# Grouped-query decode attention on one Trainium2 core: first K tile in quarters, shorter TensorE register code, a second unused matmul per V tile

## The chip, the cores and the metric

The kernel runs on one NeuronCore of a Trainium2 chip. The metric is device time of the whole kernel in microseconds (us), the median over several executions.

## The reference

One query position, 32 query heads, 8 K/V heads, 65,536 keys of 128 numbers, all bfloat16:

```python
B, Hq, Hkv, Sq, Sk, D = 1, 32, 8, 1, 65536, 128
k = jnp.repeat(k, rep, axis=1); v = jnp.repeat(v, rep, axis=1)
scores = jnp.einsum("bhqd,bhkd->bhqk", q, k) * D ** -0.5
p = _softmax(scores, axis=-1)
return jnp.einsum("bhqk,bhkd->bhqd", p, v)
```

K and V together are 268.4 MB, each byte read once. The output is 8 KB.

## The kernel before

Each of the 8 groups (one K/V head, 4 query heads) has two K tiles and two V tiles of 128 partitions x 256 keys x 128 numbers, 8.39 MB each. The kernel keeps three tiles on chip: one V tile and two K tiles. SyncE issues all loads into one queue, in the order k(0,0), k(0,1), k(1,0), v(0,0), k(1,1), v(0,1), k(2,0), ... where v(0,1) is the second V tile of group 0. A load can be issued only when the tile before it in its buffer has been used:

```python
k_lo = {0: [0, 128], 1: [0, 64, 128, 192]}
def load_k(g, b):
    SP.wait((s_sc, 16 * g - 8 + 8 * b if g else 0))     # that K buffer's scores are done
    ...
    cuts = [0, 128, SL] if g == 0 else [0, 64, 128, 192, SL] if (g, b) == (G - 1, 1) else [0, SL]
    for lo, hi in zip(cuts, cuts[1:]):
        load(k, g, b, 1 + b, s_k[b, lo], lo, hi)

def load_v(g, b):
    done = 2 * (2 * g + b)
    ...                                  # last tiles in pieces (cut)
        values_done(done)                # waits for the matmuls of the V tile before
        load(v, g, b, 0, s_v[0])
```

VectorE transposes a K tile in four quarters (64 keys each). Each quarter gives TensorE two *parts* of eight matmuls. The part loop lives in registers:

```python
with block("pe_part"):
    nc.regs_alu(r_q, r_q, 8, op=ALU.add)
    for r, bits in r_q_bits.items():              # 8, 112, 24, 96
        nc.regs_alu(r, r_q, bits, op=ALU.bitwise_and)
    ...
    take(pe, PE, s_kt, 1)
    ...                                           # eight matmuls into acc (cut)
    nc.regs_alu(r_n, r_q, 56, op=ALU.bitwise_and)
    nc.br_cmp(r_n, 56, "pe_part", "pe_skip", "IS_LT", engines=only)
...
with block("pe_values"):
    ...
    for ch in range(4):                           # quarters of a V tile, 16 wide (512-column) matmuls each
        ...
        if ch == 1:
            i.then_inc(s_vc, 1)
            pe.matmul(out=pt[0:16, :], lhsT=et[:, 0, 0:16], rhs=et[:, 0, :], start=True, stop=True)  # unused
```

After a K tile's parts, TensorE does the V tile of the group before. The very last V tile arrives in eight pieces; TensorE ends with 8 wide matmuls for the piece that ends at key 224 of each partition, and 32 small ones for the last 32 keys.

## Time and profile before

The median of the first three runs was 631.91 us (631.76 to 631.94). The profiled execution took 631.43 us.

From the page of the kernel before: busy time and share of the span per engine; then the DMA row (busy tenths of the sixteen DMA engines in 40 equal slices of the span); then the input queue (packets, MB, share of sixteen engines' span).

```profile
span 629.5 us, 7271 instructions
PE 348.6 (55%) x2126; PEld 137.9 (22%) x2126; DVE 345.3 (55%) x154; ACT 34.4 (5%) x26; POOL 9.7 (2%) x42
...
DMA  8999999999999999999999999999999999999995
...
q1 hardware_dynamic: 6656, 268.45, 98.8%
```

The DMA engines are the bound: they are busy 98.8% of the span, while TensorE and VectorE work 55% of the time. If the stream's pace stays what it is (434 GB/s, below), this kernel can win only at three places: where the stream starts, where it has a hole, and in the tail after the last bytes. So look for a hole. VectorE waits for each K tile to land, so the starts of its transposes show the stream's pace. The timeline of VectorE, before (start us, duration us, engine, line, operation; in brackets the idle time before it):

```profile
100.39 8.77 DVE L369 STREAM_TRANSPOSE io<-io 128x4096 uint32<-128x4096 uint32 x2 [14.13 <-DVEq L119]
...
140.51 17.42 DVE L369 STREAM_TRANSPOSE io<-io 128x4096 uint32<-128x4096 uint32 x4 [4.42 <-DVEq L119]
...
179.19 8.77 DVE L369 STREAM_TRANSPOSE io<-io 128x4096 uint32<-128x4096 uint32 x2 [21.09 <-DVEq L119]
```

From one K tile to the next is two loads (a V and a K tile). From 140.51 to 179.19 it is 38.68 us, and so on to the end of the run, which is 434 GB/s (16.78 MB in 38.68 us). But from 100.39 to 140.51 it is 40.12: 1.4 us more, once. The load between them that matters is v(0,1). The timeline of SyncE's DMA issues, before:

```profile
38.64 0.43 SPq L137 DMA_DIRECT2D io<-in_v_dram  x1
59.50 0.33 SPq L137 DMA_DIRECT2D io<-in_k_dram  x1
97.44 0.33 SPq L137 DMA_DIRECT2D io<-in_v_dram  x1
97.82 0.43 SPq L137 DMA_DIRECT2D io<-in_k_dram  x1
129.21 0.33 SPq L137 DMA_DIRECT2D io<-in_v_dram  x1
```

v(0,1) is issued at 97.44, and the load ahead of it, the last one queued, lands at 100.25. The trace records a completion for each of the sixteen DMA engines. For v(0,1) the first engine completes on time, at 119.21, the last only at 120.99; from then on the engines stay about 1.8 us apart to the end (1.78 at 120.99, 1.67 at 624.87), and the kernel waits for the slowest. Of the first packets of v(0,1), fourteen start by 99.79, and two start at 99.92 and 100.49 and take 2.98 and 3.29 us instead of 2.42. So this is a hole in one or two engines, and the page's DMA rows do not show it.

The tail, in the timeline of TensorE and its followers, before:

```profile
622.30 1.03 PE L254 MATMUL acc<-io,et 128*16 128x512 bf16 x8 [1.36 <-DMA io<-in_v_dram]
...
623.21 2.82 PE L354 MATMUL pf<-io,et 128*4 128x128 bf16 x28
...
626.09 0.39 PE L354 MATMUL pf<-io,et 128*4 128x128 bf16 x4
626.58 0.36 ACT L483 ACTIVATE o<-pf,rl 4x128 bf16<-4x128 f32 x1 [32.53 <-PE pf L354]
```

and the same stretch in windows of 2 us (columns: window, its length, busy us and instructions of PE, PEld, DVE, ACT, POOL; then the granted TensorE clock, which is the share of full speed that TensorE was allowed, the DMA share and GB/s):

```profile
620.00:622.00 2.00, 0.94 (x16) 0.22 (x10) 0.00 (x0) 0.00 (x0) 0.00 (x0) 1.00 1.00 379
622.00:624.00 2.00, 1.70 (x18) 1.13 (x19) 0.62 (x1) 0.00 (x0) 0.00 (x0) 0.53 0.58 198
624.00:626.00 2.00, 2.00 (x25) 1.98 (x23) 0.86 (x4) 0.00 (x0) 0.00 (x0) 0.61 0.06 18
```

The last bytes land at 624.87; TensorE ends at 626.48, 1.61 us later, because its clock was granted only by half from 622.13 to 625.55: the small matmuls start 107 ns apart in that stretch, and 56 ns apart after it.

### The profile page before, as it was taken

The numbers are of one execution on the slowest core, as the hardware profiler recorded it, in microseconds if no ns is written. First come the engines' busy times: TensorE is split into PE (matmuls) and PEld (weight loads), VectorE is DVE, ScalarE is ACT, GpSimd is POOL, SyncE is SP. The second block draws the span as 40 slices with busy tenths as digits, with TensorE's granted clock in tenths as the row PEclk, the third lists the DMA queues.
The fourth block names the chain that finished last, engine by engine and source line by source line (L and its number), as shares of the span: only waits on it lengthen the run. The fifth ranks groups of instructions, "written<-read, shape, count | busy, mean of one in ns | idle before, by whom it ended". The sixth has DMA issues, their size and how long they took to land. (4 is left out here: it accounts for less than half of the span.)

```text
span 629.5 us, 7271 instructions
## 1 busy us (share of the span) xinstructions
PE 348.6 (55%) x2126; PEld 137.9 (22%) x2126; DVE 345.3 (55%) x154; ACT 34.4 (5%) x26; POOL 9.7 (2%) x42
## 2 busy tenths in 40 slices
PE   0776384827628275381854718458183671886435
PEld 0222131312213122130311303123031230332113
DVE  4994846549065590655807557084670946694210
ACT  0000200020000200002000020000200002000100
POOL 2000000000000000000000000000000000000000
PEclk9999596976959789596896968869698695999567
DMA  8999999999999999999999999999999999999995
GB/s 367 433 466 400 466 400 462 404 462 404 462 408 458 408 458 408 458 408 458 408 458 412 454 412 454 416 450 429 437 433 433 441 425 441 401 428 433 433 431 237
DMA packets 6715, 268.48 MB, mean 426 GB/s; under 512 B 825, under 2 KB 1081, under 8 KB 1465
## 3 DMA queue, kind: packets, MB, share of 16 engines
q1 hardware_dynamic: 6656, 268.45, 98.8%
q8 instruction: 1, 0.02, 0.0%
q10 hardware_dynamic: 56, 0.01, 0.0%
q14 instruction: 2, 0.01, 0.0%
HBM read 268.44 MB, written 0.01 MB: 426 GB/s over the span
## 5 line engine op out<-in xcount | busy, mean ns | idle before, releaser
L296 PE MATMUL acc<-io,wz 128*128 x1024 | 268.7, 413 | 192.7 <-PEq L119 185.6
L369 DVE STREAM_TRANSPOSE io<-io 128x4096 uint32<-128x4096 uint32 x64 | 279.6, 4415 | 154.0 <-DVEq L119 154.0
L296 PEld LDWEIGHTS acc<-io,wz 128*128 x1024 | 105.2, 103 | 356.3 <-issue 276.5
L254 PE MATMUL acc<-io,et 128*16 128x512 bf16 x1016 | 68.1, 412 | 20.8 <-PEq L119 19.4
L406 DVE TENSOR_REDUCE mg<-acc 128x1 f32<-128x2048 f32 x8 | 18.3, 2292 | 54.1 <-DVEq L119 54.1
L436 ACT ACTIVATE ex<-acc,nmb 128x2048 bf16<-128x2048 f32 x8 | 15.7, 1967 | 557.6 <-DVE nmb L416 557.6
L254 PEld LDWEIGHTS acc<-io,et 128*16 128x16 bf16 x1016 | 26.2, 94 | 59.2 <-issue 35.3
L248 PE MATMUL pf<-vs,sel 128*4 128x130 f32 (+1 forms) x20 | 5.7, 386 | 54.2 <-PEq L119 54.2
L372 DVE STREAM_TRANSPOSE et<-ex 128x1024 bf16<-128x1024 bf16 x17 | 20.8, 1225 | 22.2 <-SPq L157 12.4
L446 ACT ACTIVATE acc<-wz 128x2560 f32<-128x2560 bf16 (+2 forms) x8 | 16.3, 2040 | 1.0 <-ACT ex L436 0.2
L505 POOL COPY wz<-qT 32x16 bf16<-32x16 bf16 x32 | 6.1, 189 | 514.1 <-PE acc L296 442.8
L408 DVE TENSOR_REDUCE m<-pt 1x4 f32<-1x128 f32 x8 | 2.2, 279 | 21.0 <-DVEq L119 21.0
L248 PEld LDWEIGHTS pf<-vs,sel 128*4 128x4 f32 x20 | 1.2, 83 | 54.7 <-issue 54.7
L380 DVE TENSOR_REDUCE vs<-vy 128x128 f32<-128x512 f32 x9 | 6.1, 681 | 7.6 <-DVEq L119 7.6
L419 DVE TENSOR_TENSOR vy<-acc,sely 128x512 f32<-128x512 f32 x8 | 8.5, 1064 | 0.0
L468 DVE TENSOR_TENSOR vy<-acc,sely 128x512 f32<-128x512 f32 x1 | 0.7, 692 | 12.1 <-PE acc L254 12.1
L321 PE MATMUL pt<-et 128*16 128x512 bf16 x16 | 6.5, 406 | 0.0
L338 PE MATMUL pb<-ident,nrow 1*128 1x1 f32 x8 | 1.6, 200 | 7.5 <-PEq L119 7.5
L336 PE MATMUL pt<-ident,mg 128*1 128x128 f32 x8 | 2.3, 283 | 2.6 <-PEq L119 2.6
L416 DVE COPY nmb<-pb 128x1 f32<-128x1 f32 x8 | 1.3, 158 | 4.0 <-DVEq L119 4.0
L354 PE MATMUL pf<-io,et 128*4 128x128 bf16 x32 | 3.2, 281 | 0.0
L338 PEld LDWEIGHTS pb<-ident,nrow 1*128 1x128 f32 x8 | 1.2, 144 | 8.9 <-issue 8.9
(31 smaller groups left out, 22.9 us busy)
## 6 DMA issues: line engine op xcount, KB each, us to landing
io<-in_v_dram SPq DMA_DIRECT2D x5, 4096.0 KB, 16.8
io<-in_k_dram SPq DMA_DIRECT2D x4, 4096.0 KB, 26.0
io<-in_k_dram SPq DMA_DIRECT2D x4, 2048.0 KB, 40.2
io<-in_v_dram SPq DMA_DIRECT2D x1, 2048.0 KB, 10.8
io<-in_v_dram SPq DMA_DIRECT2D x1, 1024.0 KB, 13.0
io<-in_v_dram SPq DMA_DIRECT2D x3, 256.0 KB, 13.3
io<-in_v_dram SPq DMA_DIRECT2D x2, 128.0 KB, 13.3
io<-in_k_dram SPq DMA_DIRECT2D x13, 48.0
```

The source lines that it names most:

```text
L248: return pe.matmul(out=pf[0:H, 0:w], lhsT=sel[:, :], rhs=vs[:, 0:w], skip_group_check=True, **kw)
L254: return pe.matmul(out=vacc[32 * c:32 * c + 16, :, :], lhsT=et[:, ch // 2, w0:w0 + 16], rhs=io[:, PS * ch + 4 * tt:PS * ch + 4 * tt + 4, : ...
L296: i = pe.matmul(out=bass.AP(acc, r_o, [[2560, P], [1, 512]]), lhsT=bass.AP(wz, r_w + ((2 * s + e) * WB - 4 * u), [[4 * WB, P], [1, P]]), r ...
L321: pe.matmul(out=pt[0:16, :], lhsT=et[:, 0, 0:16], rhs=et[:, 0, :], start=True, stop=True)
L369: dve.transpose(out=part, in_=part).then_inc(s_kt, 2)
L372: dve.transpose(out=et[:, :, :].rearrange("p i n -> p (i n)"), in_=ex[:, 2 * b:2 * b + 2, :].rearrange("p i n -> p (i n)"),).then_inc(s_et, 1)
L380: DV.mark(dve.tensor_reduce(out=vs[:, 0:D], in_=vy[:, :, :], axis=AX.X, op=ALU.add))
L406: dve.tensor_reduce(out=mg[:, :], in_=sc, axis=AX.X, op=ALU.max).then_inc(s_mg, 1)
L419: dve.tensor_tensor(out=vy[:, :, :].rearrange("p d y -> p y d"), in0=vacc, in1=sely[:, :, None].to_broadcast([P, 4, D]), op=ALU.mult,).the ...
L436: act.activation(out=ex[:, :, :].rearrange("p b n -> p (b n)"), in_=sc, func=ACT.Exp, bias=nmb[:, :], scale=SCALE, accum_out=vs[:, D + g % ...
L446: act.activation(out=part, in_=wz[:, 0, 0:1].to_broadcast([P, part.shape[1]]), func=ACT.Copy).then_inc(s_cl, 1)
L505: gp.tensor_copy(out=wz[r, :, c0:c0 + H].rearrange("p (s w) h -> p s w h", s=2), in_=qTb[r, :, :, g, :],).then_inc(s_w, 1)
```

## The change

It has three separate parts. (a) The first K tile is loaded in quarters, so that TensorE can start sooner. (b) TensorE's part loop is compared with a tile's last part through one counting register, with fewer register operations. (c) A second unused matmul is done at three quarters of a V tile, beside the one at two quarters.

```diff
-    k_lo = {0: [0, 128], 1: [0, 64, 128, 192]}
+    k_lo = [0, 64, 128, 192]
...
-        cuts = [0, 128, SL] if g == 0 else [0, 64, 128, 192, SL] if (g, b) == (G - 1, 1) else [0, SL]
+        cuts = k_lo + [SL] if (g, b) in ((0, 0), (G - 1, 1)) else [0, 128, SL] if g == 0 else [0, SL]
...   (the semaphores of the pieces are credited by GpSimd in group 1, not by SyncE)
-    r_q_bits = {...: b for b in (8, 112, 24, 96)}
+    r_q_bits = {...: b for b in (8, 16, 96)}
...
-        r_k = n8 * (2 * D // 8) + m8 * (PS * D // 16) + SL * D
-        r_w = w8 * (-1) + 28
-        r_o = o8 * 16
+        r_k = n8 * (2 * D // 8) + (n16 + c) * (PS * D // 16) + SL * D
+        r_w = (n8 + n16) * (-1) + 28
+        r_o = c * 16
...
-        nc.regs_alu(r_n, r_q, 56, op=ALU.bitwise_and)
-        nc.br_cmp(r_n, 56, "pe_part", "pe_skip", "IS_LT", engines=only)
+        nc.br_cmp(r_q, r_z, "pe_part", "pe_skip", "IS_LT", engines=only)
...
             if ch == 1:
                 i.then_inc(s_vc, 1)
+            if ch in (1, 2):
                 pe.matmul(                          # unused
```

## The prediction

> **What bounds it now.** The DMA engines. The table of DMA queues gives the input queue 98.8% of sixteen engines' span. In the timeline, transposes of one K tile start every 77.41 us per group (217.89, 295.30, 372.69...): 33.55 MB in 77.41 us is 433 GB/s; [...]. TensorE and VectorE (55% each) have slack. So only the stream's start, a hole in it, and the tail can count.
>
> **The hole.** The recorded landings of whole tiles are 19.35 us apart, except once. k of group 1 half 1 lands at 100.25 (sixteen engines within 0.4 us); the next tile, v of group 0 half 1, has its first engine at 119.21 (no hole) but its last at 120.99. The engines stay 1.8 us apart to the end. That v load was issued at 97.44, only 2 us before the engines ran out (99.4); in the packet records two engines start its first packet late (99.92, 100.49), and these packets take 2.98 and 3.29 us instead of 2.42. One engine loses about 1.4 us, and the end waits for the slowest. The k load issued at 38.15, 3.7 us ahead, caused no such spread; later loads are issued 7 us or more ahead.
>
> **What the change does.** The issue at 97.44 waits for group 0's v matmuls, after a chain from the first tile: TensorE starts at 18.26 because the first half lands at 13.1, and its parts (8 matmuls, 2.57 us warm) end at 59.4, 8 us after the last transpose.
> - Quarters: first landing near 8.2, first part near 13.4; first tile finished near 34 instead of 38.15. The second tile still lands at 32.5 and 42.2, and TensorE may go cold before it, so the group ends only 1 to 2.3 us earlier (estimate).
> - Registers: per part three short operations fewer, one fused one more; issues are 93 to 97 ns apart, so 0.1 to 0.15 us per part, 0.8 us or more over group 1's first tile. In steady state hidden.
> - One more unused matmul per v tile: 0.21 us warm, 0.43 cold (estimates from matmul spacing); hidden except in the last tile.
> - Moved semaphore increments: nothing.
>
> So the v load should go out near 95, enough to remove most or all of the hole: about 1.4 us.
>
> **The tail.** After the landing at 622.26 TensorE does 8 wide and 32 small matmuls in 4.2 us at half clock (granted 0.5 from 622.13), then the output. The clock changes fall on a 3.41 us grid [...]. The window before 622.13 was a third busy. The extra matmul and the 1.4 us shift can make it busy enough for full clock; the small matmuls (107 ns cold) would then take about 60. Worth 0 to 1.2 us; a coin toss.
>
> **Prediction.** 631.9 - 1.4 - 0.4 = 630.1 us, range 629.1 to 631.5. Faster by over 2%: 0.5%; within 2%: 99%; slower: 0.5%.
>
> **What would show it.** First part near 13.4; that v load issued near 95; landings 19.35 apart with the engines' spread near 0.4 us to the end; last landing near 623.5 instead of 624.87; the steady rate unchanged; parts near 2.45 us warm; the granted clock after 620.
>
> **What would make it wrong.** The v load still less than 3 us ahead (hole stays: 631.5 to 632); another hole from the small first loads; a warm tail with no hole (629); the clock grid falling otherwise.

## The result, and the profile after

The changed kernel took 629.81 us (629.47 to 630.29, six runs) against 631.51 us (630.61 to 631.94) over six runs of before. The ratio is 0.9975, with a 95% interval of 0.9962 to 0.9988. Ratios here are the mean time of one kernel's runs over that of the other's of the same rounds, so not quite the ratio of the medians quoted. All outputs are right. The prediction was 630.1 us, 629.1 to 631.5.

The page after, the lines that answer to those shown of before:

```profile
span 627.7 us, 7067 instructions
PE 356.4 (57%) x2142; PEld 139.8 (22%) x2142; DVE 345.5 (55%) x154; ACT 34.4 (5%) x26; POOL 9.7 (2%) x42
...
DMA  8999999999999999999999999999999999999996
...
q1 hardware_dynamic: 6944, 268.45, 99.2%
```

TensorE even has more busy time, as it does 16 more unused matmuls and runs at a lower mean clock (0.796 against 0.807). The DMA share rose from 98.8 to 99.2%: the same bytes in less span. SyncE's issues after:

```profile
33.28 0.43 SPq L137 DMA_DIRECT2D io<-in_v_dram  x1
57.31 0.33 SPq L137 DMA_DIRECT2D io<-in_k_dram  x1
95.12 0.33 SPq L137 DMA_DIRECT2D io<-in_v_dram  x1
```

v(0,1) now goes out at 95.12 instead of 97.44. The transposes after:

```profile
100.66 8.77 DVE L373 STREAM_TRANSPOSE io<-io 128x4096 uint32<-128x4096 uint32 x2 [16.42 <-DVEq L119]
...
139.36 17.43 DVE L373 STREAM_TRANSPOSE io<-io 128x4096 uint32<-128x4096 uint32 x4 [3.36 <-DVEq L119]
...
178.07 8.77 DVE L373 STREAM_TRANSPOSE io<-io 128x4096 uint32<-128x4096 uint32 x2 [21.12 <-DVEq L119]
```

Both steps are 38.7 us now: the hole is gone, and the engines stay 0.49 us apart until 507 us (0.8 from there on). The tail, in the timeline and in the windows, after:

```profile
621.48 1.03 PE L254 MATMUL acc<-io,et 128*16 128x512 bf16 x8
...
622.39 1.94 PE L359 MATMUL pf<-io,et 128*4 128x128 bf16 x28
...
624.40 0.39 PE L359 MATMUL pf<-io,et 128*4 128x128 bf16 x4
624.89 0.36 ACT L487 ACTIVATE o<-pf,rl 4x128 bf16<-4x128 f32 x1 [31.54 <-PE pf L359]
```

```profile
620.00:622.00 2.00, 1.88 (x21) 0.41 (x14) 0.00 (x0) 0.00 (x0) 0.00 (x0) 0.50 0.99 375
622.00:624.00 2.00, 2.00 (x35) 1.64 (x27) 1.37 (x4) 0.00 (x0) 0.00 (x0) 0.80 0.65 215
624.00:626.00 2.00, 0.79 (x12) 0.54 (x9) 0.10 (x2) 0.36 (x1) 0.00 (x0) 1.00 0.02 4
```

The last bytes land at 624.11, only 0.76 us earlier than before, and TensorE ends 0.68 us after that instead of 1.61. The two add up to 1.69 of the 1.8 us between these two spans (629.54 and 627.73). The clock was at half here too, from 612.55 to 622.79; the full clock came back in time for most of the small matmuls, while before it had just been lost, at 622.13.

### The profile page after: what moved, and what is told of

Read it like the earlier page. It is cut to its first block, busy times and chain, and to the rows that moved or that the text cites. A ratio compares the mean times of both kernels' runs of the same rounds, so it can differ in the third digit from the quotient of the medians.

```text
span 627.7 us, 7067 instructions
## 1 busy us (share of the span) xinstructions
PE 356.4 (57%) x2142; PEld 139.8 (22%) x2142; DVE 345.5 (55%) x154; ACT 34.4 (5%) x26; POOL 9.7 (2%) x42
## 3 DMA queue, kind: packets, MB, share of 16 engines
q1 hardware_dynamic: 6944, 268.45, 99.2%
## 5 line engine op out<-in xcount | busy, mean ns | idle before, releaser
L301 PE MATMUL acc<-io,wz 128*128 x1024 | 272.7, 420 | 184.8 <-PEq L119 157.3
L254 PE MATMUL acc<-io,et 128*16 128x512 bf16 x1016 | 72.5, 416 | 19.3 <-PEq L119 19.2
L254 PEld LDWEIGHTS acc<-io,et 128*16 128x16 bf16 x1016 | 27.7, 94 | 58.4 <-issue 35.5
L326 PE MATMUL pt<-et 128*16 128x512 bf16 x32 | 13.1, 411 | 0.0
L326 PEld LDWEIGHTS pt<-et 128*16 128x16 bf16 x32 | 3.1, 97 | 4.5 <-issue 1.4
```

The source lines that it names most:

```text
L254: return pe.matmul(out=vacc[32 * c:32 * c + 16, :, :], lhsT=et[:, ch // 2, w0:w0 + 16], rhs=io[:, PS * ch + 4 * tt:PS * ch + 4 * tt + 4, : ...
L301: i = pe.matmul(out=bass.AP(acc, r_o, [[2560, P], [1, 512]]), lhsT=bass.AP(wz, r_w + ((2 * s + e) * WB - 4 * u), [[4 * WB, P], [1, P]]), r ...
```

## The experiments

Theory: the gain comes from v(0,1) being issued early enough, plus the clock in the tail. Rivals: the shorter loop pays by itself all through the run; the faster start pays by itself; the unused matmul and the tail's clock are the whole gain. Twelve runs were made; e11 and e12 repeat the two kernels of the change. All were timed against before, e6 and e7 in three rounds, the others in five. Before itself had medians of 631.31 us (rounds of e1 to e4), 631.23 (e5 to e8) and 631.49 (e9 to e12), with single executions from 629.93 to 633.04; the three sets of rounds ran on different chips, so compare by the ratios first.

This table has what each trace shows of the stream. *Issue*: of v(0,1), or of its first part. *Lead*: the landing of the load ahead, k(1,1), minus the issue. *Lost*: the time between the landings of k(1,1) and v(0,1) (last engine each) over the usual 19.35 us. *Last*: the last landing. *Tail*: the end of TensorE's work minus the last landing. All are us, from the trace's records of DMA landings and instructions.

| kernel | issue | lead | lost | last | tail | median (range) | ratio to before, 95% interval |
|---|---|---|---|---|---|---|---|
| before | 97.44 | 2.81 | 1.39 | 624.87 | 1.61 | 631.51 (630.61-631.94) | |
| changed | 95.12 | 5.40 | 0.00 | 624.11 | 0.68 | 629.81 (629.47-630.29) | 0.9975 (0.9962-0.9988) |
| e1 quarters only | 95.68 | 4.69 | 0.00 | 624.11 | 0.67 | 629.74 (629.35-630.50) | 0.9971 (0.9957-0.9986) |
| e2 registers only | 95.90 | 4.53 | 0.00 | 624.16 | 0.66 | 630.19 (629.66-631.44) | 0.9980 (0.9965-0.9995) |
| e3 unused only | 97.75 | 2.64 | 1.69 | 625.94 | 0.67 | 631.42 (630.25-631.89) | 0.9990 (0.9975-1.0006) |
| e4 changed, no quarters | 95.75 | 4.44 | 0.01 | 624.42 | 1.68 | 629.98 (629.57-631.04) | 0.9974 (0.9959-0.9988) |
| e5 changed, one unused | 94.66 | 5.71 | 0.00 | 624.25 | 0.66 | 630.05 (629.33-630.90) | 0.9982 (0.9967-0.9997) |
| e6 changed, load held 2 us | 97.18 | 3.09 | 1.55 | 625.21 | 0.65 | 630.53 (629.94-631.09) | 0.9988 (0.9970-1.0006) |
| e7 changed, load held 4 us | 98.99 | 1.36 | 1.18 | 625.25 | 0.95 | 630.63 (630.19-631.24) | 0.9989 (0.9971-1.0007) |
| e8 before, v(0,1) in halves | 95.44 | 5.30 | 0.08 | 624.54 | 0.66 | 630.22 (629.87-630.76) | 0.9984 (0.9971-0.9998) |
| e9 changed, five unused | 95.74 | 4.61 | 0.01 | 624.11 | 0.66 | 629.37 (629.24-629.50) | 0.9965 (0.9952-0.9978) |
| e10 changed, no unused | 94.31 | 6.16 | 0.18 | 624.50 | 0.67 | 629.77 (629.63-630.49) | 0.9975 (0.9962-0.9988) |
| e11 changed, again | 94.83 | 5.51 | 0.00 | 623.97 | 0.94 | 629.51 (629.34-630.19) | 0.9971 (0.9958-0.9984) |
| e12 before, again | 97.30 | 2.85 | 0.62 | 624.14 | 0.70 | 631.49 (629.77-632.97) | 1.0001 (0.9987-1.0015) |

### e1: the quarters alone

```diff
  (before)
-        cuts = [0, 128, SL] if g == 0 else ...
+        cuts = k_lo + [SL] if (g, b) in ((0, 0), (G - 1, 1)) else [0, 128, SL] if g == 0 else [0, SL]
  (and the credits of the pieces' semaphores, as in the change)
```

> Before plus the quarters alone. Theory (a late v load makes one DMA engine late): the first part starts near 13.7 us instead of 18.3; each part still takes 2.57 us, so the critical v load is issued near 96 us instead of 97.4, 3.5 us or more ahead of the engines' running out; the engines' spread at that v landing stays under 0.8 us instead of 1.8; stream costs 0.27 us more at the start, as in the changed kernel. Time 0.5 to 1.3 us under before. Rival 1 (the shorter loop does it, quarters nothing): v load still near 97.4, spread 1.8, same time. Rival 2 (the gain is only the tail's clock, from the unused matmul): same time as before within 0.4 us.

The first part started at 13.47 and v(0,1) went out at 95.68. The spread there stayed at 0.37 us, though it grew to 0.82 later, for a reason told below. The time was 629.74 us, as fast as the whole change. It is 1.6 us under before's median of the same rounds, more than the 0.5 to 1.3 expected. The expected cost of 0.27 us at the start was not there: k(0,1) landed at 42.31, and in the traces with halves at 42.04 to 42.37, so what I had read in the first pair of traces (42.20 and 42.48) was scatter. Rivals 1 and 2 fail as sole causes: this kernel has neither the shorter loop nor the second unused matmul.

### e2: the register code alone

```diff
  (before)
-    r_q_bits = ... (8, 112, 24, 96)
+    r_q_bits = ... (8, 16, 96)
-        nc.regs_alu(r_n, r_q, 56, op=ALU.bitwise_and)
-        nc.br_cmp(r_n, 56, "pe_part", "pe_skip", "IS_LT", engines=only)
+        nc.br_cmp(r_q, r_z, "pe_part", "pe_skip", "IS_LT", engines=only)
  (and the rest of the register part of the change)
```

> Before plus the shorter register code alone. Theory: parts take about 2.45 us instead of 2.57 when warm; TensorE starts at 18.3 as before but lags less, so the first group ends near 57.7 instead of 59.4 and the critical v load goes out near 95.5; the spread stays near 0.4 us, and there is no extra cost of small first loads: last landing near 623.6, time 1 to 1.6 us under before. If the quarters are what is needed: v load still after 97, spread over 1.5, time within 0.3 us of before.

TensorE started at 18.53, as late as before, but caught up. Its timeline, first of the kernel before and then of e2, shows the start of one part after another:

```profile
26.01 1.91 PE L296 MATMUL acc<-io,wz 128*128 x8 [0.68 <-PEq L119]
28.59 1.90 PE L296 MATMUL acc<-io,wz 128*128 x8 [0.67 <-PEq L119]
```

```profile
28.43 1.91 PE L301 MATMUL acc<-io,wz 128*128 x8 [0.58 <-PEq L119]
30.88 1.91 PE L301 MATMUL acc<-io,wz 128*128 x8 [0.54 <-issue]
```

A part takes 2.45 us instead of 2.58; the matmuls are the same 1.9 us, and the pause between parts is shorter. v(0,1) went out at 95.90 (expected 95.5), with no hole. The time fell by about 0.2% (ratio 0.9980). The last landing, 624.16, missed the 623.6 expected. So the registers alone suffice too: either part of the change removes the hole, and the second has nothing left to remove.

### e3: the second unused matmul alone

```diff
  (before)
+            if ch in (1, 2):
```

> Before plus the second unused matmul alone. Theory: v load issued 0.2 us later (97.6), the hole stays (spread 1.8 us or a little more, last landing near 624.9 to 625.1); the tail between the landing of the piece at three quarters and the output may go warm: 0 to 0.9 us less. Time 0 to 0.9 us under before. Rival 2 (the tail's clock is the whole gain): 1.5 us under before or more.

v(0,1) went out at 97.75, the hole was 1.69 us, the largest of all. In this trace all engines lost another 0.6 us or so between 121 and 200 us (landings 19.44 to 19.62 us apart), which no other trace shows so large; the cause is open, and it makes the last landing miss its expectation. The tail was at full clock (0.67 us). The time shows no gain, but its interval reaches down to 0.9975, the ratio of the whole change, so the time alone excludes nothing. What the trace shows is that the second unused matmul does not remove the hole; e5 and e10, which keep a gain without it, show that it is not needed.

### e4: the change without the quarters

```diff
  (changed kernel)
-        cuts = k_lo + [SL] if (g, b) in ((0, 0), (G - 1, 1)) else [0, 128, SL] if g == 0 else [0, SL]
+        (as before: halves)
```

> The changed kernel without the quarters (registers and unused matmul stay). If the register code alone brings the v load early enough (near 95.7), the stream has no hole and is 0.27 us shorter than in the changed kernel, as the first load is in halves: last landing near 623.6 to 623.8, time 1.7 to 2.2 us under before, so as fast as the changed kernel or up to 0.4 us faster. If the quarters are needed: spread over 1.5 us, last landing near 624.9, time 0.9 us under before at best.

v(0,1) at 95.75, no hole, 629.98 us: the quarters are not needed beside the register code. The last landing (624.42) missed: all engines together lost 0.34 us between 119.6 and 158.6 us, of the same unexplained kind as in e3, and 0.6 us near the end, at a packet told of below. This profile had a tail at half clock *with* both unused matmuls:

```profile
620.00:622.00 2.00, 0.79 (x13) 0.20 (x9) 0.00 (x0) 0.00 (x0) 0.00 (x0) 0.99 0.98 376
622.00:624.00 2.00, 2.00 (x24) 1.58 (x17) 1.12 (x2) 0.00 (x0) 0.00 (x0) 0.50 0.72 246
```

That refutes the idea that the second unused matmul secures the clock.

### e5: the change with one unused matmul per V tile

```diff
  (changed kernel)
-            if ch in (1, 2):
+            if ch == 1:
```

> The changed kernel without the second unused matmul. Theory: the v load goes out 0.2 us earlier (94.9), no hole, last landing 624.1 as in the changed kernel; the tail after it is 0.7 us if the clock is granted in full then and 1.6 if not, which the phase of the 3.41 us grid decides in each execution; the run with quarters alone was warm without the second unused matmul, so no clear loss here: time within 0.3 us of the changed kernel (629.5 to 630.3). If the second unused matmul is what gives the full clock: half clock after 622 in this profile and 0.5 to 0.9 us more.

As the theory said: issue 94.66, no hole, a tail at full clock with one unused matmul, 630.05 us with a range that covers the changed kernel's.

### e6: the changed kernel, v(0,1) held back by about 2 us

```diff
  (changed kernel)
+            if (g, b) == (0, 1):
+                SP.wait((s_late, 7))
             load(v, g, b, 0, s_v[0])
...  (GpSimd, end of group 1's turn)
+        if g == 1:
+            GP.wait((s_vc, 2))
+            for i in range(7):
+                GP.wait((s_late, i))
+                gp.memset(idle[:, :], 0.0).then_inc(s_late, 1)   # 240 unused elements
+            GP.wait((s_late, 7))
```

> The changed kernel with that v load held back on purpose: GpSimd does seven small memsets of unused space one after another once the v matmuls of group 0 are done, and the load waits for the last, about 2.3 us. Everything else stays. Theory: issue near 97.4, about 2.2 us ahead of running out, as before the change; spread at that landing 1.4 to 2.3 us and to the end, last landing 624.9 to 625.7, time 0.6 to 1.4 us over the changed kernel's (630.5 to 631.4). Rival (the lead of this load does not matter; the gain came from elsewhere): no spread, time as the changed kernel.

This is the direct test, as it keeps the fast start and the short loop and moves only this issue and that of k(2,0) right behind it. SyncE's issue and VectorE's transposes in e6:

```profile
97.18 0.33 SPq L139 DMA_DIRECT2D io<-in_v_dram  x1
```

```profile
100.41 8.77 DVE L377 STREAM_TRANSPOSE io<-io 128x4096 uint32<-128x4096 uint32 x2 [16.52 <-DVEq L121]
...
140.65 17.42 DVE L377 STREAM_TRANSPOSE io<-io 128x4096 uint32<-128x4096 uint32 x4 [4.90 <-DVEq L121]
```

The step is 40.24 us again, and the engines stay 1.7 us apart to the end. The time was 630.53 us, 0.7 us over the changed kernel's first median and 0.5 us over e5 in rounds on the same chip, with ranges that overlap. The interval of its ratio still reaches 1, so the trace, not the time, carries the verdict: the late issue brings the hole back, and the rival without a role for the lead falls.

### e7: the same, held back by about 4 us

```diff
-                SP.wait((s_late, 7))
+                SP.wait((s_late, 12))
```

> The same with twelve memsets, about 4 us: issue near 99, under 1 us ahead of running out. Theory: all engines run dry here, not one or two: the first engine's landing is late too (over 0.5 us), the last one 2.5 to 4 us later than in the changed kernel; time 2 to 3.5 us over it (631.8 to 633.5). Rival: as the changed kernel.

Here the theory's size was wrong. All engines did run dry, but they lost only 1.18 us together and stayed 0.5 us apart; the time was 630.63 us, not 631.8 or more. In this trace all sixteen engines start the first packet of v(0,1) between 99.94 and 100.59, 0.95 to 1.6 us after the issue at 98.99. In the trace of before the latest engine started 3.05 us after the issue. So the loss did not grow with lateness here (1.18 us against 1.39): a load that reached fourteen engines in time left one engine worse off than a load that reached all sixteen after they had run dry. A late start is only a part of the loss. All sixteen first packets took 2.66 to 3.31 us here instead of 2.42, and in every trace with a late issue some did (up to 3.11 us in e3, 3.74 in e6, and 3.26 in e12 on an engine that started on time, at 99.57); with an early issue none took over 2.61. Why one engine is served so late, and why such packets are slow, stays open.

### e8: before, with only v(0,1) loaded in halves

```diff
  (before)
-        elif (g, b) in ((G - 2, 1), (G - 1, 0)):
+        elif (g, b) in ((0, 1), (G - 2, 1), (G - 1, 0)):
  (and its semaphore's credits moved to match)
```

> The kernel before, and only this v tile loaded in two halves, the first half of it as soon as the first half of the tile before is used (none of the three parts of the change). Theory: first half issued near 95.4, second near 97.4 with 9.7 us of data queued ahead, so no hole: spread stays near 0.4 us, landing near 119.8 to 120.0, last landing 623.5 to 624.1, time 0.8 to 1.7 us under before, as much as the whole change brings. Rival (it is the faster start or the shorter loop that pays): time as before.

None of the three parts of the change is here. The first half is issued as soon as the first half of the V tile before has been used:

```profile
59.55 0.33 SPq L137 DMA_DIRECT2D io<-in_k_dram  x1
95.44 2.33 SPq L137 DMA_DIRECT2D io<-in_v_dram  x2
97.82 0.43 SPq L137 DMA_DIRECT2D io<-in_k_dram  x1
```

The transposes in e8, and the step between them, 38.78 us:

```profile
100.88 8.77 DVE L371 STREAM_TRANSPOSE io<-io 128x4096 uint32<-128x4096 uint32 x2 [14.61 <-DVEq L119]
...
139.66 17.42 DVE L371 STREAM_TRANSPOSE io<-io 128x4096 uint32<-128x4096 uint32 x4 [3.07 <-DVEq L119]
```

The hole is gone (0.08 us lost, by all engines alike), and the time, 630.22 us, is 0.16% under before by the ratio. The gap to the changed kernel (0.4 us in medians of different rounds) is inside the noise of these intervals. So the rival that only a faster start or loop can remove the hole falls as well; that the time gain is the whole change's is not shown. The last landing, 624.54, missed the expected 623.5 to 624.1: all engines lost 0.4 us earlier, between 42.3 and 81.4 us, which is unexplained, and 0.4 us at the packet near the end.

### e9: five unused matmuls per V tile

```diff
  (changed kernel)
-            if ch in (1, 2):
+            for _ in range({1: 3, 2: 2}.get(ch, 0)):
```

> The changed kernel with three unused matmuls at two quarters of a v tile and two at three quarters (one each in the changed kernel), so that TensorE hardly pauses in the last v tile. Theory: v load issued near 95.7 (0.6 us later, still 3.5 us or more ahead): no hole, last landing 624.0 to 624.3. TensorE busy from 614 to 622.5 with no pause over 0.5 us, which holds one whole 3.41 us window whatever its phase, so full clock from 621 at the latest; last small matmul 0.6 to 0.8 us after the last landing. Time 629.3 to 629.9, the changed kernel or 0.3 us under it on average. If the extra work only gets in the way: three-quarter matmuls start 0.5 us late and nothing is gained.

All numbers came as expected but one: TensorE paused once for 0.94 us (620.52 to 621.46), where no pause over 0.5 was expected. The windows of e9:

```profile
620.00:622.00 2.00, 1.06 (x16) 0.24 (x11) 0.00 (x0) 0.00 (x0) 0.00 (x0) 1.00 0.98 367
622.00:624.00 2.00, 1.81 (x31) 1.35 (x26) 1.47 (x4) 0.00 (x0) 0.00 (x0) 1.00 0.61 202
```

The clock was whole through the tail, and the five timed executions lie within 0.26 us, the narrowest range of all. Its median, 629.37 us, is the lowest, and it beats before clearly (ratio 0.9965). It is not shown to beat the changed kernel: in the same rounds that had 629.51 us, and the intervals overlap for the most part.

### e10: no unused matmul

```diff
  (changed kernel)
-            if ch in (1, 2):
-                pe.matmul(out=pt[0:16, :], ...)
```

> The changed kernel without any unused matmul. If unused matmuls matter for the tail: half clock for most small matmuls of the tail, last one 1.5 us after the last landing, time 0.5 to 0.9 us over the changed kernel. If the phase of the grid alone decides, as the runs so far suggest (full clock there in four of five profiles with one unused matmul, three of five with two): either state in this profile, time within 0.4 us of the changed kernel. Hole: none in either case, v load issued near 94.5.

v(0,1) at 94.31, full clock in the tail, 629.77 us. So this one profile needed no unused matmul either. The 0.18 us lost is no hole in one engine: all sixteen first packets took 2.48 to 2.59 us.

### e11 and e12: both kernels once more

> The changed kernel once more, for a second trace of it beside the second trace of before: v load near 95.1 and spread under 0.6 us there again; last landing 623.9 to 624.3; the clock grid falls otherwise, so the tail after it may take 0.7 or 1.6 us. Time 629.4 to 630.3.

> The kernel before once more: v load near 97.4, spread 1.5 to 2.4 us from there to the end, last landing 624.7 to 625.7, tail 0.7 or 1.6 us by the phase of the grid. Time 630.0 to 632; a fast execution near 630 would be one with the hole and a warm tail.

e11 confirms the first trace: issue 94.83, nothing lost, last landing 623.97; its tail was in between (0.94 us), as the full clock came at 623.33. Its spread, 0.37 us after v(0,1), met the expectation there but grew to 0.65 later. e12 brought a miss that teaches: with the issue at 97.30 only 0.62 us was lost, not 1.5 or more, and with a full-clock tail this execution of the *unchanged* kernel took 629.77 us, as fast as the changed one. Its other five took 630.32 to 632.97. So the hole is a lottery of 0.6 to 1.7 us in the traces with a late issue, and the tail a second lottery of about 1 us; the change takes the first away. No trace was taken of an execution over 632 us, so what those lose is open. The traces also account for only a part of the gain in the times: the last landing is at 624.24 us on average in the nine traces with an early issue and at 625.04 in the four with a late one, 0.8 us apart, while the medians of the two kernels are 1.7 to 2.0 us apart. Where the rest comes from is not shown.

## Why the prediction was right

The time was right (629.81 against 630.1, inside the range), and the mechanism of the hole was confirmed in the traces. But two terms of the sum were off and cancelled, so that it came out this close is partly luck.

- *"So only the stream's start, a hole in it, and the tail can count."* Right. The steady pace did not change (landings 19.35 us apart in both kernels), although parts became shorter all through the run.
- *"So the v load should go out near 95, enough to remove most or all of the hole."* Right: 95.12. The steps to it also came: first part at 13.68 (13.4 said), first tile's buffer reissued at 32.91 (34 said), group 0 done about 2.2 us earlier (1 to 2.3 said), parts of 2.45 to 2.49 us (2.45 said). Causation is shown from both sides: e6 puts the late issue back and gets the hole back, e8 advances the issue without the change and loses the hole. Over all traces, the four issued 2.6 to 3.1 us ahead lost 0.6 to 1.7 us, and the nine issued 4.4 us or more ahead lost 0.2 or less (e7, 1.4 us ahead, lost 1.18 on all engines). The margin can be narrowed: k(1,0), the load that the prediction names as safe, was issued 3.9 us before the landing ahead of it in before, e3 and e12, and 0.03 us or less was lost. What I did not foresee is that (a) and (b) each suffice.
- *"about 1.4 us"*: mis-sized as a gain at the end. At v(0,1) the hole was 1.39 us and went to zero, but the last landing came only 0.76 us earlier, and in the second pair (e11, e12) 0.17. In the first pair, 0.28 us went at the start (k(0,1) landed at 42.48 instead of 42.20, scatter as e1 showed), and 0.3 us was lost again between 507 and 527 us, where the engines' spread grew from 0.50 to 0.80. *"The engines' spread near 0.4 us to the end; last landing near 623.5"* was wrong for this reason. At 518.16 the trace has one 8 KB packet on an instruction queue, 0.31 us long. In each of the ten traces with nothing large lost on a single engine, the spread grows by 0.3 to 0.6 us at the first landing after that packet, wherever it falls (362 us in e7, 516 to 518 with quarters otherwise, 615 to 616 with halves). In the traces with a hole on one engine it shows no such step. So removing the hole seems to lay this cost bare: with one engine 0.8 to 2.3 us behind, the others had slack for it. That the packet holds up one data engine is a reading of these coincidences, not an experiment.
- *"Worth 0 to 1.2 us; a coin toss"* for the tail, entered as 0.4: it was 0.93 in the first pair (1.61 to 0.68), which made up for the other term. But the tail is not a steady gain of the change: 0.24 the other way in the second pair (0.70 and 0.94).
- *"The extra matmul and the 1.4 us shift can make it busy enough for full clock."* This is not what happened in the first pair. The changed kernel did not keep a full clock into the tail: it was at half clock until 622.79, and regained it after the window from 619.38, which was 0.97 busy. Where the clock's grid lay in that execution gave the short tail, and that was luck (in e11, the same kernel, the full clock came at 623.33 and the tail was 0.94 us). Nor is the full clock secured by one more matmul: e4 had it and ran at half clock, e10 had none and ran at full. In e9, with five, TensorE was 65% busy in the window before the tail and kept its clock.

The traces show this of the clock. Cutting all fourteen into the grid of 3.413 us on which the clock changes (all changes of a trace fall on it within 2 ns), and summing TensorE's matmul time in each window (ends are modelled, so shares are rough): at full clock, every window busy 0.42 or less was followed by half clock, every one busy 0.50 or more by full clock, with both outcomes in between; at half clock, full clock followed only windows busy 0.76 or more. The last V tile of before had 0.36 in the window from 618.72, and e4's had 0.40; the two that kept the clock least safely there had 0.43 (e8) and 0.45 (e1). The grid does not start with the kernel: the first change was at 21.39 us in before and at 18.64 after, 2.75 us apart, which is not a whole window.

That the stream can go no faster than the 434 GB/s measured between K tiles (16.78 MB in 38.68 us) was not shown; no run tested it. At that pace, about 624 us of last landing plus 0.7 us of tail plus the output is my estimate, from the table above, of what this design can reach; e9 (624.11 and 0.66) is at it.

## What to carry to other kernels

When the DMA engines bind (98.8% of the span here), look for the one load that is issued just before the queue runs dry, and look engine by engine: in before, an engine of sixteen that started its first packet late (at 100.49) went with 1.39 us lost at v(0,1), though the mean busy share hides it. In these runs any change upstream that moved that issue about 1.5 us or more ahead removed the hole, and doing it in two ways paid no more than in one, within the noise, so try the parts alone. For a short tail on TensorE, look at how busy it is in the window of 3.413 us ahead if its full clock matters (in these traces it kept the full clock after windows busy 0.50 or more), and judge such a gain by many executions, as one profile shows one draw.
